# Transposing nine large groups by DMA, linear sums in four banks per group, coefficients without a clip, and a new order

## The chip, the core and the metric

The program runs on one core of one Trainium2 chip. The metric is the device time of one execution in microseconds (us), lower is better. One execution was profiled; its times, and a measured time beside its span, are what the numbers below come from.

## What is computed

`x` has 4 batches of 12480 rows of 128 values, `inducing` is 32 x 128. Per batch, 32 inducing rows attend over all 12480 rows (giving `h`, 32 x 128), then every row attends over the 32 rows of `h`, and the result goes through a two-layer network with a hard swish.

```python
def mab(q, kv):
    s = scale * (q @ kv.transpose(0, 2, 1))
    s = s - s.max(-1, keepdims=True)
    a = np.exp(s)
    a /= a.sum(-1, keepdims=True) + 1e-09
    return a @ kv
h = mab(I, x)                          # (4, 32, 128)
x2 = mab(x, h).reshape(49920, 128)
h2 = x2 @ w_in                         # w_in 128 x 2048
g = h2 * np.clip(h2 + 3.0, 0.0, 6.0) / 6.0
out = g @ w_out                        # 49920 x 128, float32
```

## The kernel before

A row's second attention is a weighted mean of 32 rows of `h`, so `h2` is the same mean of 32 rows of `G = h @ w_in`. While all of `G` lies within 3 of zero, the clip does nothing, and `out` is a quadratic form in the 32 weights: linear terms in the 32 weights squared by `e`, and products of two weights, with coefficients of 128 values each. The kernel computes per batch the coefficients (`Cq` for products, `BD` for linear terms) and per row the products, and multiplies. At the end it counts on the chip whether every assumption held (`y0` to `y5`, `bad_i`); if not, a slow direct path would run instead.

Rows of a batch come in **six large groups** of 2048 rows (g = 0 to 5) and one small group of 192 (g = 6). A large group is 16 tiles of 128 rows: 4 classes j by 4 tiles s. The program is written as a table of tokens, `ORDER`, a code with its arguments (batch b, group g, half h, PSUM bank k, engine V, A or P); the table alone sets the order on each engine, and each engine works through its own instructions strictly in that order. The eight PSUM banks are given by number in the tokens; the rings in SBUF by counting (`xh` 7, `xT` 13, `TF` 3, `TD` 2, `d` 3, `os` 2).

The steps of one large group, with the lines of before:

- `X` (L416, from POOL's queue): loads 2048 rows to `xh`, float32 to float16. `T` (L422): 8 transposes of 128 x 128 on TensorE for half a group, `Y` (L428): the copy of one bank to `xT` on DVE or ACT. `T` and `Y` stand twice per group.
- First attention: `S` (L433) scores, `E` (L441) exponential, `A` (L449, L459) sums, `H` (L476).
- After the last group of a batch, the coefficients: `c3` to `cB`, `G` (L523), `cG` (L532) writes `GL`, `cH` on POOL (L543) clips to `r6`, `cI` (L548) multiplies, `L`, `cL`, `cM`, `cm`, `cN` (L595, `BD` with a mask), `p` (L609), `P` (L616), `cP`, `cX`, `cY` (`Cq`). `cJ` (L553, DVE) takes the largest `G`.
- Second attention: `Z` (L656) scores, `Zz` (L678), `Zd` (L666), `Ze` (L671), `ee` (L692), `R`, `Rr`, `R2`. `W` (L698, four per group, SP's queue) copies `dk` to `d` with each partition's row on four partitions.
- Products, per half of a group: `B` (L731, tiles of 32 rows of the array, four banks), `F` (L741, ACT) to `TF`, `U` (L750, DVE) `TD = TF * d`.
- Sums: `q` (L789, 128 x 128 x 128 matmuls on `TF` and `TD`) and `l` (L770, tiles of 64 rows, 256 columns) into one bank for each half h and pair of classes jp, `v` (L807 on DVE, L811 on ACT) scales the bank's 512 columns into `os`, `O` (L817, SP's queue) stores `os`.

SP's queue thus holds `W` and `O`, POOL's queue `X` and the weights. Batches overlap: the first attention of batch b+1 stands among the products of batch b.

Of the kernel before, what the change touches and what calls it, by code (L numbers as in the profile page):

```python
# [9 lines left out]
FP32 = mybir.dt.float32  # L10
# [10 lines left out]
it X.0.1.0.16 i2 i1 w.2.0 i3.V T.0.1.0.8.1 Y.0.1.0.8.1.V i0 w.2.5 w.2.2 X.0.0.8.16 T.0.0.8.16.1 w.2.7 Y.0.0.8.16.1.V  # L21
i4.5 X.0.0.0.8 T.0.0.0.8.0 w.2.1 T.0.1.8.16.4 X.0.3.0.16 T.0.3.8.16.3 Y.0.0.0.8.0.A i5.5.V S.0.0.8.16.2 Y.0.1.8.16.4.A
X.0.2.0.16 T.0.3.0.8.0 Y.0.3.8.16.3.V Y.0.3.0.8.0.A E.0.0.8.16.2 S.0.0.0.8.6 i8 S.0.1.0.16.3 w.2.0 X.0.4.0.16 i6
A.0.0.8.16.7 H.0.0.8.16.7 T.0.2.0.8.2 w.2.1 E.0.0.0.8.6 A.0.0.0.8.6 w.2.4 T.0.2.8.16.4 Y.0.2.8.16.4.V Y.0.2.0.8.2.A
E.0.1.0.16.3 wi.0 wh.1.V A.0.1.0.16.2 S.0.3.0.16.3 E.0.3.0.16.3 X.0.5.0.16 T.0.4.0.8.0 Y.0.4.0.8.0.A H.0.1.0.16.2 i9
T.0.4.8.16.4 Y.0.4.8.16.4.V S.0.2.0.16.5 E.0.2.0.16.5 H.0.0.0.8.6 X.0.6.0.2 A.0.3.0.16.2 wh.0.A wl.0.V A.0.2.0.16.5
S.0.4.8.16.6 S.0.4.0.8.1 wi.1 T.0.5.8.16.4 T.0.6.0.2.3 T.0.5.0.8.0 E.0.4.0.8.1 Y.0.6.0.2.3.V S.0.6.0.2.7 Y.0.5.0.8.0.V
A.0.4.0.8.3 H.0.3.0.16.2 H.0.4.0.8.3 Y.0.5.8.16.4.A X.1.1.0.16 S.0.5.8.16.4 wh.2.V E.0.6.0.2.7 S.0.5.0.8.1 wh.3.V
E.0.5.8.16.4 X.1.0.0.16 wo.1 A.0.6.0.2.0 H.0.6.0.2.0 A.0.5.8.16.4 wo.0 E.0.4.8.16.6 A.0.4.8.16.7 H.0.5.8.16.4
E.0.5.0.8.1 H.0.4.8.16.7 H.0.2.0.16.5 A.0.5.0.8.6 H.0.5.0.8.6 c3.0.0 wl.3.V T.1.1.0.8.5 c7.0.V wl.1.P c8.0.V  # L30
T.1.1.8.16.4 i7.P G.0.1.2 wl.2.P G.0.3.2 G.0.2.2 Y.1.1.8.16.4.A c4.0.0 c9.0 cB.0.P G.0.0.2 cK.0 Z.0.2.1.7 Zd.0.2.7 cA.0
Z.0.0.0.1 Y.1.1.0.8.5.V cG.0.2 Z.0.0.1.5 Zd.0.0.5 W.0.0.0 W.0.0.2 Z.0.1.1.3 Zz.0.0.1 Z.0.1.0.2 Zd.0.1.3 Zz.0.1.2 W.0.0.1
cD.0.0.V T.1.0.8.16.0 T.1.0.0.8.4 X.1.3.0.16 cH.0.P cD.0.1.A Y.1.0.8.16.0.V S.1.1.0.16.6 Y.1.0.0.8.4.A W.0.0.3
E.1.1.0.16.6 Z.0.3.0.5 Z.0.2.0.7 cI.0 Zz.0.2.7 p.0.2.V W.0.2.3 B.0.0.0.2.0 S.1.0.0.16.4 F.0.0.0.0.2 E.1.0.0.16.4 L.0.0.6
A.1.1.0.16.7 W.0.2.0 H.1.1.0.16.7 L.0.1.6 cL.0.6 p.0.1.V A.1.0.0.16.4 cM.0.0.6 W.0.1.0 Ze.0.0 cm.0.3 ee.0.0.V cN.0.3
# [148 lines left out]
def kernel(  # L184
# [35 lines left out]
    with ExitStack() as es:  # L220
# [537 lines left out]
        def begins(b, g, h, jp):  # L758
            new = (b, g, h, jp) not in open_
            open_.add((b, g, h, jp))  # L760
            return new
# [269 lines left out]
```

## Time and profile before

| | |
|---|---|
| median of three timed runs (lowest, highest) | 249.86 us (248.54, 251.14) |
| the profiled execution, its time and its span | 249.51 us, 247.5 us |
| TensorE matmul (PE) busy | 227.0 us, 92% |
| VectorE (DVE) busy | 202.4 us, 82% |
| ScalarE (ACT) busy | 191.1 us, 77% |
| GpSimd (POOL) busy | 40.3 us, 16% |
| DMA | 53.91 MB, mean 218 GB/s |
| first and last `q` matmul | 47.4 us, 240.9 us |

A row of a group of instructions reads: line, engine, operation, out<-in, shapes, count, then busy us and mean ns of one, then the engine's idle time just before them and what ended it. A matmul's duration includes its way through the array; successive matmuls overlap, so what one costs is the distance from start to start. In a row of a window the columns are busy us with the number of instructions in brackets for PE, PE's weight loads (PEld), DVE, ACT and POOL, then the granted clock, the busy share of the DMA engines, and GB/s.

### The profile page before, as it was taken

How to read it: one execution, taken by the hardware profiler on the slowest of the kernel's cores; microseconds unless marked ns; L12 is line 12 of the kernel's file. 1: busy time of each engine (PE TensorE's matmuls, PEld its weight loads, DVE VectorE, ACT ScalarE, POOL GpSimd, SP SyncE). 2: the span in 40 equal slices, each digit the busy share in tenths (PEclk: the TensorE clock that was granted, in tenths of full speed). 3: DMA queues.
4: the chain of work that ended last, by engine and by line, in shares of the span. 5: the costliest groups of instructions: out<-in, count | busy, mean ns of one | idle time of the engine just before them, and what ended most of it. 6: DMA issues, size and time to landing. Idle time of an engine off the chain costs nothing. (4 is left out here: it accounts for less than half of the span.)

```text
span 247.5 us, 10076 instructions
## 1 busy us (share of the span) xinstructions
PE 227.0 (92%) x4317; PEld 186.5 (75%) x4317; DVE 202.4 (82%) x438; ACT 191.1 (77%) x350; POOL 40.3 (16%) x80
## 2 busy tenths in 40 slices
PE   1879799999799999999899999999999999989990
PEld 0568758888698798797787888888878877768780
DVE  0236879989599997999778998988889999998983
ACT  2167277998788886999687786999889889989870
POOL 8518582021002500010004000000031000000000
PEclk9999679999999999999999999999999999999998
DMA  6999789969989999849879974623981849696953
GB/s 96 193 255 254 238 158 193 208 163 250 214 286 263 277 196 331 293 87 250 184 252 265 266 274 110 224 56 76 338 305 37 262 97 340 211 311 170 362 232 134
DMA packets 23744, 53.91 MB, mean 218 GB/s; under 512 B 3697, under 2 KB 16785, under 8 KB 20753
## 3 DMA queue, kind: packets, MB, share of 16 engines
q1 hardware_dynamic: 19072, 38.36, 47.4%
q0 software_dynamic: 4624, 14.88, 31.0%
q8 instruction: 34, 0.56, 0.8%
q14 instruction: 14, 0.11, 0.1%
HBM read 27.67 MB, written 25.56 MB: 215 GB/s over the span
## 5 line engine op out<-in xcount | busy, mean ns | idle before, releaser
L741 ACT ACTIVATE TF<-ps 128x1024 f16<-128x1024 f32 (+1 forms) x100 | 96.8, 1007 | 16.1 <-PE ps L731 12.4
L750 DVE TENSOR_TENSOR TD<-TF,d 128x2048 f16<-128x2048 f16 (+1 forms) x52 | 59.9, 1156 | 3.0 <-ACT TF L741 2.2
L789 PE MATMUL ps<-Cq,TF 128*128 128x128 f16 (+1 forms) x784 | 57.9, 219 | 2.6 <-issue 1.4
L789 PE MATMUL ps<-Cq,TD 128*128 128x128 f16 (+1 forms) x784 | 56.0, 219 | 0.0
L807 DVE TENSOR_TENSOR os<-ps,r 128x512 f32<-128x512 f32 x68 | 45.4, 683 | 11.7 <-PE ps L789 4.1
L789 PEld LDWEIGHTS <-TF 128*128 128x128 f16 (+1 forms) x784 | 46.3, 98 | 6.3 <-issue 6.0
L789 PEld LDWEIGHTS <-TD 128*128 128x128 f16 (+1 forms) x784 | 46.1, 99 | 4.3 <-issue 3.4
L811 ACT ACTIVATE os<-ps,r 128x128 f32<-128x128 f32 x112 | 32.0, 380 | 4.3 <-PE ps L789 2.0
L422 PE MATMUL ps<-ident_h,xh 128*128 128x128 f16 x384 | 29.8, 226 | 5.5 <-DMA xh<-in_x_dram 5.5
L422 PEld LDWEIGHTS <-xh 128*128 128x128 f16 x384 | 24.0, 102 | 11.6 <-DMA xh<-in_x_dram 7.5
L428 DVE COPY xT<-ps 128x1024 f16<-128x1024 f16 x31 | 21.2, 684 | 12.8 <-PE ps L422 12.5
L428 ACT COPY xT<-ps 128x1024 f16<-128x1024 f16 x17 | 17.0, 1015 | 18.9 <-PE ps L422 18.8
L416 POOL DMA_DIRECT2D xh<-in_x_dram x25 | 13.9, 560 | 75.1 <-PE ps L459 62.2
L731 PE MATMUL ps<-z,pair 32*128 32x256 f16 (+1 forms) x400 | 20.3, 270 | 0.0
L609 DVE TENSOR_TENSOR PR<-Gd 128x2048 bf16<-128x2048 bf16 x16 | 19.8, 1239 | 0.0
L678 DVE TENSOR_SCALAR_CACHE_REDUCE z<-ps 128x512 f16<-128x512 f32 (+1 forms) x28 | 17.3, 621 | 2.4 <-PE ps L656 2.3
L666 ACT ACTIVATE dk<-ps 128x512 f16<-128x512 f32 (+1 forms) x28 | 14.8, 547 | 5.5 <-PE ps L656 3.4
L770 PE MATMUL ps<-BD,ee 64*128 64x256 f16 (+1 forms) x196 | 17.5, 273 | 0.2
L441 ACT ACTIVATE a<-ps 128x512 f16<-128x512 f32 (+1 forms) x27 | 14.6, 556 | 2.6 <-PE ps L433 2.6
L616 PE MATMUL ps<-w_ob,PR 128*128 128x128 bf16 x256 | 16.5, 219 | 0.0
L671 ACT ACTIVATE e<-z 128x512 f16<-128x512 f16 (+1 forms) x28 | 16.3, 589 | 0.1
L616 PEld LDWEIGHTS <-PR 128*128 128x128 bf16 x256 | 14.7, 98 | 0.9 <-issue 0.8
(137 smaller groups left out, 284.8 us busy)
## 6 DMA issues: line engine op xcount, KB each, us to landing
out_dram<-os SPq DMA_DIRECT2D x23, 1024.0 KB, 5.2
d<-dk SPq DMA_DIRECT2D x96, 128.0 KB, 3.9
xh<-in_x_dram POOLq DMA_DIRECT2D x23, 512.0 KB, 8.8
os<-in_moe_w_in_dram POOLq DMA_DIRECT2D x2, 512.0 KB, 13.4
w_or<-in_moe_w_out_dram POOLq DMA_DIRECT2D x2, 512.0 KB, 11.6
out_dram<-os SPq DMA_DIRECT2D x2, 512.0 KB, 3.6
xh<-in_x_dram POOLq DMA_DIRECT2D x2, 256.0 KB, 7.3
out_dram<-osl SPq DMA_DIRECT2D x4, 96.0 KB, 3.0
```

The source lines that it names most:

```text
L422: nc.tensor.transpose(pt[:, (i - lo) * p : (i - lo + 1) * p], at(xh, xhl, b, g)[:p, i, :], ident_h[:p, :p])
L428: copier(e)(xT_of(b, g)[:, lo * p : hi * p], ps[:, k, :].bitcast(FP16)[:, : (hi - lo) * p])
L609: veng(e).tensor_mul(pr_of(b, c)[:, :, :].rearrange("p a (i m) -> p a i m", m=M), views[0], views[1])
L616: nc.tensor.matmul(ps[:, k, f * C : (f + 1) * C], lhsT=pr_of(b, c)[:, jb, :], rhs=w_ob[:, jb, :], start=first_of(b, u), stop=False, skip_g ...
L678: nc.vector.tensor_scalar(fat(z_, b, g)[:rows, :w], ps[:rows, k, :w], 1.0, None, op0=ALU.mult, op1=ALU.min, accum_out=z_all[:rows, b * NGR ...
L731: nc.tensor.matmul(ps[:, pairs[j // 2] + j % 2, f * w : (f + 1) * w], lhsT=pair[rows, f, :], rhs=fat(z_, b, g)[rows, h * w : (h + 1) * w], ...
L741: nc.scalar.activation(hat(TF_, b, g, h)[:, 2 * q : 2 * q + 2, :w], ps[:, k : k + 2, :w], ACT.Exp, scale=scale / KH)
L750: nc.vector.tensor_mul(split(hat(TD_, b, g, h)), split(hat(TF_, b, g, h)), d.unsqueeze(2).to_broadcast([P, J, 2, w]),)
L770: nc.tensor.matmul(ps[:p, ks[jp], s2 * 2 * C : (s2 + 1) * 2 * C], lhsT=fat(e2_, b, g)[rows, s * p : (s + 1) * p], rhs=BD_[b % 2][rows, :, ...
L789: nc.tensor.matmul(ps[:p, k, (s2 * 2 + j2) * C : (s2 * 2 + j2 + 1) * C], lhsT=t[:, j, f * w + s2 * p : f * w + (s2 + 1) * p], rhs=Cq_[b % ...
L807: nc.vector.tensor_mul(o, src, r.unsqueeze(3).to_broadcast([p, Sh, 2, C]))
L811: nc.scalar.mul(o[:, s2, j2, :], src[:, s2, j2, :], r[:, s2, j2 : j2 + 1])
```

## The change

It does four things.

1. **Transposes by DMA.** For nine of the 24 large groups (2.1, 2.3, 2.4, 2.5, 3.1 to 3.5; batch and group) the two `T` and two `Y` go, and one token `t` comes: a DMA transpose of the whole group, `xh` to `xT`, in SP's queue. 18 of 48 large `T` and `Y` go: 15 of those `Y` stood on DVE, 3 on ACT.
2. **Linear sums of a whole group.** `l` is called once per large group: 16 matmuls of 32 rows and 128 columns, one array tile and one bank for each class j, in place of two calls of 4 matmuls of 64 rows and 256 columns. `q` writes each class to its own bank, so a group's sums stand in four banks, both halves side by side, until a `v` per class reads 512 columns.
3. **No clip.** `cH` and `r6` go, `cI` computes (G + 3) G at once; `cJ` becomes a sum of squares on ACT (with the bound 9 in place of 3 on the largest). The mask in `BD` goes.
4. **New order.** `ORDER` is another table; matmuls that only keep TensorE awake are 12 in place of 16, and seven copies to `Gd` stand on ACT in place of four.

The core of the diff:

```diff
 ORDER = """
-... T.2.3.8.16.3 ... Y.2.3.8.16.3.V ...
+... t.2.3 ...
+        def op_t(b, g):
+            nc.sync.dma_start(
+                xT_of(b, g)[:, :].rearrange("c (i t) -> c i t", t=P),
+                at(xh, xhl, b, g)[:, :, :].rearrange("t i c -> t (i c)"),
+                transpose=True,
+            )
...
-        def op_cH(b, e):
-            veng(e).tensor_scalar(
-                r6[:, :, :], GL[:, :, :M].bitcast(FP32), 3.0, 0.0, op0=ALU.add, op1=ALU.max
-            )
-
         def op_cI(b):
             nc.vector.scalar_tensor_tensor(
-                GL[:, :, M:], r6[:, :, :], 6.0, GL[:, :, :M].bitcast(FP32), op0=ALU.min, op1=ALU.mult
+                GL[:, :, M:],
+                GL[:, :, :M].bitcast(FP32),
+                3.0,
+                GL[:, :, :M].bitcast(FP32),
+                op0=ALU.add,
+                op1=ALU.mult,
             )
 
         def op_cJ(b):
-            nc.vector.tensor_reduce(
-                g_all[:, b : b + 1],
+            nc.scalar.activation(
+                junk[:, :].rearrange("p (a m) -> p a m", m=M),
                 GL[:, :, :M].bitcast(FP32),
-                axis=AX.XY,
-                op=ALU.max,
-                apply_absolute_value=True,
+                ACT.Square,
+                accum_out=g_all[:, b : b + 1],
             )
...
+        def op_l(b, g, *ks):
+            t0, p, J, Sn = groups[g]
+            for s in range(Sn):
+                for j in range(J):
+                    rows = slice(32 * j, 32 * j + 32)
                     nc.tensor.matmul(
-                        ps[:p, ks[jp], s2 * 2 * C : (s2 + 1) * 2 * C],
+                        ps[:p, ks[0] + j if g == NG else ks[j], s * C : (s + 1) * C],
                         lhsT=fat(e2_, b, g)[rows, s * p : (s + 1) * p],
-                        rhs=BD_[b % 2][rows, :, :].rearrange("p j c -> p (j c)"),
-                        start=begins(b, g, h, jp),
+                        rhs=BD_[b % 2][rows, :],
+                        start=begins(b, g, j),
                         stop=False,
                         skip_group_check=True,
-                        tile_position=(64 * jp, 0),
+                        tile_position=(32 * j, 0),
                     )
...
-        def op_q(b, g, h, jp, u, k):
+        def op_q(b, g, h, jp, u, *ks):
...
-                            ps[:p, k, (s2 * 2 + j2) * C : (s2 * 2 + j2 + 1) * C],
+                            ps[:p, ks[0] + j2 if g == NG else ks[j2], (h * Sh + s2) * C : (h * Sh + s2 + 1) * C],
...
-        def op_v(b, g, h, jp, k, e):
+        def op_v(b, g, j, k, e):
...
-                nc.vector.tensor_mul(o, src, r.unsqueeze(3).to_broadcast([p, Sh, 2, C]))
+                n = js.stop - js.start
+                nc.vector.tensor_mul(o, src, r.unsqueeze(3).to_broadcast([p, n, Sn, C]))
```

**SP's queue while batch 1 is multiplied out.** The first piece is of before, from the store of group 0.5 on; L698 is `W` (`d`), L817 is `O` (`os`), 96 at a row's end is the small group.

```order
L817 DMA out_dram<-os_118 128x2048
L698 DMA d_111<-dk_108 128x1x512 x2
L698 DMA d_110<-dk_107 128x1x512 x2
L698 DMA d_109<-dk_106 128x1x512
L698 DMA d_111<-dk_108 128x1x512 x2
L698 DMA d_110<-dk_107 128x1x512
L817 DMA out_dram<-os_117 128x2048
```

The second piece is of the change, from the store of group 0.5 on as well; L694 is `W`, L813 is `O`, and L423 is `t` (here of groups 2.3 and 2.4).

```order
L813 DMA out_dram<-os_118 128x2048
L423 DMA_TRANSPOSE xT_79<-xh_69 128x16x128
L423 DMA_TRANSPOSE xT_80<-xh_70 128x16x128
L694 DMA d_109<-dk_106 128x1x512 x3
L694 DMA d_110<-dk_107 128x1x512 x2
L813 DMA out_dram<-os_117 128x2048
```

Two transposes now stand between the store and the `W` of groups 1.2 and 1.3.

**DVE while groups 2.0 and 2.1 are multiplied out.** The first piece is of before: L807 is `v`, L428 is `Y` (`xT_85` to `xT_87` are groups 3.3 to 3.5), L750 is `U` of group 2.1, L692 is `ee`.

```order
L807 TENSOR_TENSOR os_117<-ps,r_165 128x2x256
L428 COPY xT_85<-ps 128x1024
L807 TENSOR_TENSOR os_117<-ps,r_165 128x2x256
L692 TENSOR_TENSOR ee_102<-e_99 128x512
L428 COPY xT_85<-ps 128x1024
L750 TENSOR_TENSOR TD_115<-TF_113,d_109 128x2048
L428 COPY xT_86<-ps 128x1024
L807 TENSOR_TENSOR os_117<-ps,r_165 128x2x256
L428 COPY xT_87<-ps 128x1024
```

The second piece is of the change, at the same groups: L800 is `v`, L746 is `U` of group 2.1, L475 is `H`, L688 is `ee`, L719 is `R2`.

```order
L800 TENSOR_TENSOR os_117<-ps,r_163 128x4x128 x2
L475 TENSOR_TENSOR hacc_135<-hacc_135,ps 128x33
L800 TENSOR_TENSOR os_117<-ps,r_163 128x4x128 x2
L746 TENSOR_TENSOR TD_115<-TF_113,d_109 128x2048
L475 TENSOR_TENSOR hacc_135<-hacc_135,ps 128x33
L746 TENSOR_TENSOR TD_116<-TF_114,d_109 128x2048
L688 TENSOR_TENSOR ee_100<-e_97 128x512
L688 TENSOR_TENSOR ee_102<-e_99 128x512
L719 TENSOR_TENSOR r_163<-rc_162 128x16
L800 TENSOR_TENSOR os_118<-ps,r_163 128x4x128 x4
```

The copies to `xT` are gone, and the four evictions of group 2.1 (`os_118`) stand in one run, where before those of group 2.0 (`os_117`) stood one by one between copies.

More of the change, by code (lines that the diff above doesn't have):

```diff
@@ L26 @@
[L26 to L35, printed above, removed]
@@ L153 @@
+q.3.5.1.1.0.4.5 l.3.5.0.1.4.5 W.3.6.0 y2 B.3.6.0.6 v.3.4.1.2.A O.3.4.0.16 q.3.5.0.0.1.0.1 cJ.3 q.3.5.1.0.0.0.1
+q.3.5.1.0.1.0.1 F.3.6.0.0.6 Ze.3.6 ee.3.6.V R2.3.5.V v.3.5.0.0.A v.3.5.1.1.V q.3.5.0.1.1.4.5 U.3.6.0 q.3.5.1.1.1.4.5
+q.3.5.0.1.0.4.5 R.3.6.7 Rr.3.6.7 O.3.5.0.8 v.3.5.3.5.V R2.3.6.V y1 q.3.6.0.0.1.2 q.3.6.0.0.0.2 v.3.5.2.4.A O.3.5.8.16
+l.3.6.2 v.3.6.0.2.V y0 O.3.6.0.2 y3 y4.6 y5.6
 """
@@ L247 @@
         Cq_ = ring("Cq", 2, [P, 4, C], FP16)
-        BD_ = ring("BD", 2, [P, 2, C], FP16)
+        BD_ = ring("BD", 2, [P, C], FP16)
         HS_ = ring("HS", 2, [P, M], FP16)
@@ L258 @@
         Gd = sb.tile([P, FB, 2 * M], BF16, name="Gd")
-        r6 = sb.tile([P, FB, M], FP32, name="r6")
         LV = sb.tile([2 * M, C], FP32R, name="LV")
@@ L279 @@
         ones = sb.tile([P, 1], FP32, name="ones")
-        mask = sb.tile([P, 2, C], FP16, name="mask")
         fac = sb.tile([P, 4], FP32, name="fac")
@@ L351, in op_i6 @@
                 e.memset(blk[rows, j : j + 1], math.sqrt(KC))
-                e.memset(mask[rows, j % 2, :], 1.0)
             e.memset(fac[:, :], KC / 3.0)
@@ L756, with begins @@
         open_ = set()
-        def begins(b, g, h, jp):
-            new = (b, g, h, jp) not in open_
-            open_.add((b, g, h, jp))
+        def begins(b, g, j):
+            new = (b, g, j) not in open_
+            open_.add((b, g, j))
             return new
-        def op_l(b, g, h, *ks):
+        def op_l(b, g, *ks):
             t0, p, J, Sn = groups[g]
-            Sh = (Sn + 1) // 2
-            for s2 in range(Sh):
-                s = h * Sh + s2
-                for jp in range(J // 2):
-                    rows = slice(64 * jp, 64 * jp + 64)
+            for s in range(Sn):
+                for j in range(J):
+                    rows = slice(32 * j, 32 * j + 32)
                     nc.tensor.matmul(
-                        ps[:p, ks[jp], s2 * 2 * C : (s2 + 1) * 2 * C],
+                        ps[:p, ks[0] + j if g == NG else ks[j], s * C : (s + 1) * C],
                         lhsT=fat(e2_, b, g)[rows, s * p : (s + 1) * p],
-                        rhs=BD_[b % 2][rows, :, :].rearrange("p j c -> p (j c)"),
-                        start=begins(b, g, h, jp),
+                        rhs=BD_[b % 2][rows, :],
+                        start=begins(b, g, j),
                         stop=False,
                         skip_group_check=True,
-                        tile_position=(64 * jp, 0),
+                        tile_position=(32 * j, 0),
                     )
-        def op_q(b, g, h, jp, u, k):
+        def op_q(b, g, h, jp, u, *ks):
             t0, p, J, Sn = groups[g]
@@ L816, in op_O @@
             r0 = b * N + t0
-            nc.sync.dma_start(
-                out[r0 : r0 + p * n, :].rearrange("(p i) c -> p i c", i=n)[:, lo:hi, :],
-                at(os_, osl, b, g)[:p, lo:hi, :],
-            )
+            o = out[r0 : r0 + p * n, :].rearrange("(p i) c -> p i c", i=n)
+            t = at(os_, osl, b, g)[:p]
+            if hi - lo == n:
+                nc.sync.dma_start(o, t)
+            else:
+                half = lambda a: a.rearrange("p (s j) c -> p s j c", j=J)[:, :, lo // 4 : hi // 4, :]
+                nc.sync.dma_start(half(o), half(t))
         def op_dr():
@@ L844, in op_y3 @@
         def op_y3():
-            count(3, g_all[:, :], 3.0, ALU.is_le)
+            count(3, g_all[:, :], 9.0, ALU.is_le)
             d = d_all[:, :, :].rearrange("p b m -> p (b m)")
```

269 lines of the change are left out of this document (133 added, 136 removed).

## The prediction

> **What bounds the kernel now.** I read the page's busy shares first, then busy time by stretch, then who waits for whom, then single instructions in one stretch.
>
> ```profile
> PE 227.0 (92%) x4317; PEld 186.5 (75%) x4317; DVE 202.4 (82%) x438; ACT 191.1 (77%) x350; POOL 40.3 (16%) x80
> ```
>
> The stretches are the head (up to the first `q`), two parts of the long middle stage, and the tail after the last `q`. Columns: PE, PEld, DVE, ACT, POOL, then granted clock, DMA share, GB/s.
>
> ```profile
> 0.00:47.00 47.00, 37.06 (x685) 29.12 (x686) 27.20 (x66) 25.44 (x39) 24.70 (x58) 0.93 0.93 200
> 47.00:200.00 153.00, 149.78 (x2956) 124.76 (x2953) 135.53 (x283) 128.56 (x243) 15.56 (x22) 1.00 0.78 216
> 200.00:241.00 41.00, 39.79 (x680) 32.46 (x676) 37.41 (x71) 36.46 (x69) 0.00 (x0) 1.00 0.76 257
> 241.00:247.50 6.50, 0.39 (x7) 0.14 (x5) 2.29 (x22) 0.62 (x2) 0.00 (x0) 0.84 0.40 149
> ```
>
> In the 194 us from 47 to 241, PE is busy 149.8 + 39.8 = 189.6 us (98%), DVE 172.9 (89%), ACT 165.0 (85%). The head has the fullest DMA engines (0.93).
>
> The longest waits of PE:
>
> ```profile
> PE ps L422 <- DMA xh<-in_x_dram: 5.5, 3, 4.3
> ...
> PE ps L854 <- DVE junk L831: 1.9, 1, 1.9
> ...
> PE ps L481 <- DVE hacc L476: 1.5, 1, 1.5
> ```
>
> They lie in the head, the tail and before the coefficients. So the middle stage is **bound by TensorE's own work**, with DVE and ACT close behind; whatever leaves PE there counts until one of those two sets the pace.
>
> **The change, part by part.**
>
> *Transposes that leave PE.* Durations overlap, so the price is the distance between starts, taken from runs of 8 and 16:
>
> ```profile
> 19.45 1.05 PE L422 MATMUL ps<-ident_h,xh 128*128 128x128 f16 x16
> ...
> 23.18 0.61 PE L422 MATMUL ps<-ident_h,xh 128*128 128x128 f16 x8
> ```
>
> Eight more take 0.44 us, 55 ns each. Nine groups of 16 are 144: **7.9 us** off PE, all in the middle stage.
>
> *Linear sums.* One stretch of PE's rows shows both ways:
>
> ```profile
> 228.97 0.28 PE L731 MATMUL ps<-z,pair 32*128 32x256 f16 x4
> 229.18 0.39 PE L770 MATMUL ps<-BD,ee 64*128 64x256 f16 x4
> 229.51 0.62 PE L789 MATMUL ps<-Cq,TF 128*128 128x128 f16 x8
> 229.96 0.24 PE L704 MATMUL ps<-blk,e 128*128 128x4 f16 x4
> 230.07 1.05 PE L789 MATMUL ps<-Cq,TD 128*128 128x128 f16 x16
> 231.05 0.61 PE L770 MATMUL ps<-BD,ee 64*128 64x256 f16 x8
> 231.60 0.40 PE L731 MATMUL ps<-z,pair 32*128 32x256 f16 x8
> 231.93 0.45 PE L789 MATMUL ps<-Cq,TD 128*128 128x128 f16 x5
> ```
>
> `l` before costs 229.51 - 229.18 = 0.33 us for one half alone, 231.60 - 231.05 = 0.55 us for both together: 0.55 to 0.66 us per group, about 0.60. The new shape, 16 matmuls on four tiles of 32 rows, is not in the trace. Its nearest row is `B` (L731), also four tiles of 32 rows: 8 matmuls of 256 columns in 0.33 us, way out included, as many columns per tile as the 16 of 128. That is the fast end, 0.33. The slow end: 4-column `R` matmuls (L704) start (230.07 - 229.96)/4 = 27 ns apart, so 16 starts that cannot overlap take 0.43, and with the 0.2 us that `B` needs until the next full-size matmul 0.63. I take 0.40, near `B`. Per group 0.20 less, times 24: **4.8 us**, bounds (0.55 - 0.63) x 24 = -1.9 and (0.66 - 0.33) x 24 = 7.9. Together PE loses 12.7 us (6.0 to 15.8). Four warm-up matmuls fewer lie in the head, where PE waits for loads: nothing.
>
> *Evictions and small work.*
>
> ```profile
> L428 DVE COPY xT<-ps 128x1024 f16<-128x1024 f16 x31 | 21.2, 684 | 12.8 <-PE ps L422 12.5
> ...
> L428 ACT COPY xT<-ps 128x1024 f16<-128x1024 f16 x17 | 17.0, 1015 | 18.9 <-PE ps L422 18.8
> ...
> L807 DVE TENSOR_TENSOR os<-ps,r 128x512 f32<-128x512 f32 x68 | 45.4, 683 | 11.7 <-PE ps L789 4.1 <-DMA out_dram<-os 3.5 <-ACT TF L741 2.9
> ...
> L811 ACT ACTIVATE os<-ps,r 128x128 f32<-128x128 f32 x112 | 32.0, 380 | 4.3 <-PE ps L789 2.0 <-PE ps L770 1.1 <-ACT e L671 1.0
> ...
> L553 DVE TENSOR_REDUCE g_all<-GL 128x1 f32<-128x512 f32 x4 | 2.7, 665 | 0.0
> ...
> L641 ACT ACTIVATE junk<-Cp 128x512 f32<-128x512 f16 x4 | 2.5, 635 | 0.0
> ...
> L540 ACT CAST Gd<-GL 128x512 bf16<-128x512 f32 x4 | 2.4, 618 | 1.2 <-DVE GL L532 1.2
> ...
> L543 POOL TENSOR_SCALAR r<-GL 128x512 f32<-128x512 f32 x4 | 8.6, 2143 | 7.1 <-DVE GL L532 4.1 <-DVE r L723 2.8 <-DVE hm L506 0.3
> ```
>
> DVE: 15 copies at 0.684 (-10.3), `cJ` (-2.7), two large `v` more (+1.4), about -11.6 us. ACT: 3 copies (-3.0), two large `v` fewer (8 x 0.38 = -3.0), four squares at `cQ`'s price (+2.5), three `Gd` copies (+1.9): -1.6 us. So after the change the middle stage holds about PE 176.9, ACT 163.4, DVE 161.3. The clip on POOL (8.6 us) stood between `GL` and `cI`; PE has batch work beside it (98% busy), so I count nothing, and at most 2.1 us for batch 0.
>
> *What this makes of the stage.* At PE's 98% it would take 180.5 us, 13.5 less. But ACT would then be at 91%, and in the stretch from 200 to 241, where no transposes stand and all three engines are fullest, ACT reaches 36.46/41 = 89% and DVE 91%. At 89% for ACT the stage takes 163.4/0.89 = 183.6 us, 10.4 less. I take 9.5, since four banks per group leave PE a little less room (the second rival).
>
> *The transposes in SP's queue.* Each `t` waits for its load and stands ahead of `W` and `O`, which wait behind it; behind `W` wait `U` and then `q` on `TD`.
>
> ```profile
> q1 hardware_dynamic: 19072, 38.36, 47.4%
> q0 software_dynamic: 4624, 14.88, 31.0%
> ...
> out_dram<-os SPq DMA_DIRECT2D x23, 1024.0 KB, 5.2
> d<-dk SPq DMA_DIRECT2D x96, 128.0 KB, 3.9
> ...
> out_dram<-os SPq DMA_DIRECT2D x2, 512.0 KB, 3.6
> ```
>
> The trace has no DMA transpose. A group is 512 KB. By q1's bytes (38.36 MB in 47.4% of 16 x 247.5 us, 20.4 KB per us and engine) it holds all 16 engines 1.6 us. By q1's packets (98 ns each), if it goes as 2048 pieces of 256 bytes, 2048 x 98/16 = 12.6 us. The nearest row is the 512 KB store, 3.6 us from issue to landing; I take 3 us of all engines. Nine are 27 us (14 to 113). The two queues use 78.4% of 247.5, 194 us, so the stretch from 47 to 200, 0.78 full, has 0.22 x 153 = 34 us free: 27 fit. Below 34 us the term is nothing.
>
> The Trainium skill speaks twice here. "VectorE: DVE Perf Modes", section "The three transpose paths", gives 390 ns for a 128 x 128 block on TensorE and 1309 ns by DMA, which speaks against the change; as an estimate 16 blocks would be 20.9 us, nine groups 188 us. "Advanced Engine Details and Errata", section "X-Bar Transpose (TRN2)", says that such DMAs are as fast as ordinary ones, 350 to 400 GB/s; as an estimate 1.4 us per group. By the second the term above stays nothing; by the first the first rival comes. The trace cannot decide: of the 390 ns it shows 55 in a run, since a block alone is not a block in a row, and the same may hold for the DMA.
>
> *Head and tail.* Batch 0 is loaded in another order, as many bytes ahead of its last group, with the DMA engines as full: nothing, within 2 us. The tail is the same chain of counts.
>
> *Sum.* 249.5 (247.5 span and 2.0 around it) - 9.5 = **240.0 us**. The profiled execution lies 0.35 us under the median of 249.86, which I leave out.
>
> **Rivals.**
>
> *The transposes fill the DMA engines (slower).* For it: the engines are 0.93 busy in the head and 0.78 in the stretch that gets the nine; SP already issues in bursts on the chain that ended last, two of whose issues and the store behind them are
>
> ```profile
> 172.74 0.62 SPq L698
> ...
> 173.40 0.60 SPq L698
> ...
> 174.05 5.95 DMA out_dram<-os
> ...
> 180.09 0.69 DVE os L807
> ```
>
> and DVE's eviction there waits for the store. Against it: 34 us are free, and 512 KB need 1.6 us by bytes. Past 34 us every us lengthens the stage; it turns slower than before at (34 + 9.5)/9 = 4.8 us of all engines per transpose. At 6 us: 240 + (54 - 34) = 260; at 12.6: 240 + 79 = 319.
>
> *Four banks filled and emptied together (gain gone).* Before, a bank closed after 16 `q` and its `l`; now four stay open over both halves, and `B` and `F` of the next half take the other four, so PE may wait for an eviction, 0.683 us. Once in each of 24 groups that is 16.4 us: 249.5 - 12.7 + 16.4 = 253; in every second group 245. For it: DVE's evictions now stand in runs of four. Against it: `Z`, `S`, `A` and the other group's `q` stand in between.
>
> *The gain in full.* ACT and DVE keep up at 91%, `l` is at 0.33, the clip's 2.1 us goes: 249.5 - 13.5 - 1.7 - 2.1 = 232.
>
> That nothing happens because the transposes stay on PE is excluded: nine stand in SP's queue.
>
> **Chances.** Forecast, 236 to 244: 0.44. Gain in full, under 236: 0.20. Banks, 244 to 252: 0.20. DMA engines, above 252: 0.16. The range of 231 to 252 leaves out the last case and a little below. A measurement here tells no less than about 1% from no change, so the bounds are 247.4 and 252.4: of the bank case three fifths lie above 247.4. Faster 0.44 + 0.20 + 0.08 = 0.72, same 0.12, slower 0.16.
>
> **What would show it.** The transposes: 240 matmuls of 128 x 128 left on L414's line, a landing time of 3 to 6 us for `xT<-xh`, and a DMA share between 47 and 200 below 0.95. The linear sums: from the first of 16 to the next instruction 0.33 to 0.45 us. The bound: PE still above 95% in the middle, ACT near 89%. The forecast is wrong if PE waits for `xT` before scores (late transposes), if SP stands long at a `t`, if the rows of PE's waits name `v` (L800, L804), or if the stage before the first `q` grows.

## The result, and the profile after

The change is slower: 264.13 us median (262.96 to 267.94) beside 249.29 of the kernel before on the same chip (248.54 to 251.14), ratio 1.057, 95% interval 1.047 to 1.067. The forecast was 240.0, the range 231 to 252. The profiled execution took 267.94 us, span 265.8. Ratios compare only executions within 1.5% of their kernel's fastest, while medians take all of them; the profiled executions of the change, of the kernel with no `t` and of some others lie above that.

The page's first line, and the middle in three stretches (columns as in the prediction: PE, PEld, DVE, ACT, POOL, granted clock, DMA share, GB/s). First the kernel before, in shorter stretches than the prediction looked at:

```profile
47.00:100.00 53.00, 51.63 (x1021) 44.03 (x1019) 45.99 (x96) 44.52 (x83) 7.53 (x12) 1.00 0.95 245
100.00:150.00 50.00, 48.80 (x984) 40.34 (x980) 44.48 (x92) 40.75 (x75) 4.85 (x7) 1.00 0.81 227
150.00:200.00 50.00, 49.35 (x963) 40.39 (x960) 45.06 (x98) 43.29 (x86) 3.18 (x3) 1.00 0.56 174
```

Then the change:

```profile
PE 219.5 (83%) x4365; PEld 184.2 (69%) x4365; DVE 192.3 (72%) x414; ACT 191.9 (72%) x352; POOL 30.3 (11%) x72
```

```profile
47.00:100.00 53.00, 41.07 (x790) 34.40 (x790) 33.30 (x74) 34.18 (x66) 3.45 (x8) 0.90 0.89 209
100.00:150.00 50.00, 43.42 (x956) 37.02 (x948) 38.95 (x81) 38.47 (x74) 3.12 (x7) 0.97 1.04 236
150.00:200.00 50.00, 44.33 (x881) 37.61 (x880) 38.13 (x78) 38.49 (x72) 1.22 (x1) 0.89 1.01 230
```

PE did lose work, but it now waits: 24 of the 153 us are idle, where 3 were, and around its idle spells the granted clock is lower (0.74 between 140 and 160 us, around a wait of 6.5 us), so that busy time holds less work. The DMA engines are full between 100 and 200. The free time that the prediction counted (0.22 of 153 us) lay almost all behind 100 us: between 47 and 100 the engines were 0.95 busy in the kernel before.

The queues, the landings, and all instructions of the line of `t` (durations min/median/max in ns, landings in us):

```profile
q1 hardware_dynamic: 38560, 43.08, 60.8%
...
out_dram<-os SPq DMA_DIRECT2D x23, 1024.0 KB, 5.9
d<-dk SPq DMA_DIRECT2D x96, 128.0 KB, 4.1
...
xT<-xh SPq DMA_TRANSPOSE x9, 10.3
```

```profile
L423 SPq DMA_TRANSPOSE xT<-xh x9: 3457/5687/12397, 77.5 to 178.2; - x9
...
DMA to landing us min/median/max: 5.5/10.3/16.0
```

A transpose lands 10.3 us after issue, not 3 to 6. What the prediction did not price at all is the duration in the row of L423: SP itself is held 5.7 us by one `t` in the median (60.3 us by nine), where a `W` or a store holds it 0.5 to 0.6 in the median. The single packets in the trace show 2048 pieces of 256 bytes per transpose, 36 ns each in the mean (18 in the median): 41.5 us of all 16 engines for nine, 4.6 each.

What comes of it, at one place: SP's queue, then ACT and DVE (start, duration, in brackets the idle time before and what ended it), then the waits of the whole run:

```profile
132.93 5.69 SPq L423 DMA_TRANSPOSE xT<-xh  x1
138.67 5.28 SPq L694 DMA_DIRECT2D d<-dk  x7
```

```profile
150.96 0.60 ACT L662 ACTIVATE dk<-ps 128x512 f16<-128x512 f32 x1 [7.06 <-DMA d<-dk]
```

```profile
151.00 1.23 DVE L746 TENSOR_TENSOR TD<-TF,d 128x2048 f16<-128x2048 f16 x1 [5.84 <-DMA d<-dk]
```

```profile
DVE TD L746 <- DMA d<-dk: 14.0, 5, 5.8
...
ACT dk L662 <- DMA d<-dk: 9.5, 2, 7.1
...
PE ps L783 <- ACT dk L662: 6.5, 1, 6.5
```

The `t` of group 3.1 holds seven `W` back by 5.7 us. ACT, whose `Zd` may not overwrite `dk` before the `W` has read it, and DVE's `U` wait for them, and PE's next `q` waits for ACT: 6.5 us, the longest wait of PE behind the first `q`. The hold is not all of it. The `t` itself had landed at 140.5 us, but as the `W` went out, three loads did too (POOL's queue), and the seven `W` landed 10.2 us after issue, where 4.1 is the median of the run:

```profile
140.62 1.63 POOL L408 DMA_DIRECT2D xh<-in_x_dram  x3
```

```profile
d<-dk SPq DMA_DIRECT2D x7, 128.0 KB, 10.2
```

Held back, the `W` ran into the loads; how much of the wait is hold and how much is the burst, this place alone does not show.

### The profile page after: what moved, and what is told of

It reads as the page before. It is cut to its first block, busy times and chain, and to the rows that moved or that the text cites. A ratio compares the mean times of both kernels' runs of the same rounds, so it can differ in the third digit from the quotient of the medians.

```text
span 265.8 us, 10173 instructions
## 1 busy us (share of the span) xinstructions
PE 219.5 (83%) x4365; PEld 184.2 (69%) x4365; DVE 192.3 (72%) x414; ACT 191.9 (72%) x352; POOL 30.3 (11%) x72
## 3 DMA queue, kind: packets, MB, share of 16 engines
q1 hardware_dynamic: 38560, 43.08, 60.8%
## 5 line engine op out<-in xcount | busy, mean ns | idle before, releaser
L746 DVE TENSOR_TENSOR TD<-TF,d 128x2048 f16<-128x2048 f16 (+1 forms) x52 | 59.2, 1148 | 18.4 <-DMA d<-dk 14.0
L783 PE MATMUL ps<-Cq,TF 128*128 128x128 f16 (+1 forms) x784 | 59.7, 225 | 7.3 <-ACT dk L662 6.5
L800 DVE TENSOR_TENSOR os<-ps,r 128x512 f32<-128x512 f32 x70 | 45.7, 683 | 23.7 <-DMA out_dram<-os 9.3
L783 PE MATMUL ps<-Cq,TD 128*128 128x128 f16 (+1 forms) x784 | 58.7, 222 | 1.1 <-DVE TD L746 0.6
L783 PEld LDWEIGHTS <-TF 128*128 128x128 f16 (+1 forms) x784 | 48.5, 101 | 11.7 <-issue 10.9
L783 PEld LDWEIGHTS <-TD 128*128 128x128 f16 (+1 forms) x784 | 46.8, 100 | 9.1 <-issue 6.8
L804 ACT ACTIVATE os<-ps,r 128x128 f32<-128x128 f32 x104 | 29.6, 383 | 7.1 <-DMA out_dram<-os 4.3
L420 ACT COPY xT<-ps 128x1024 f16<-128x1024 f16 x14 | 14.0, 1014 | 16.6 <-PE ps L414 16.5
L414 PE MATMUL ps<-ident_h,xh 128*128 128x128 f16 x240 | 19.6, 237 | 7.4 <-DMA xh<-in_x_dram 7.1
L727 PE MATMUL ps<-z,pair 32*128 32x256 f16 (+1 forms) x400 | 22.6, 274 | 2.4 <-ACT dk L662 2.0
L662 ACT ACTIVATE dk<-ps 128x512 f16<-128x512 f32 (+1 forms) x28 | 15.1, 560 | 10.3 <-DMA d<-dk 9.5
L414 PEld LDWEIGHTS <-xh 128*128 128x128 f16 x240 | 16.0, 107 | 8.6 <-DMA xh<-in_x_dram 7.2
L420 DVE COPY xT<-ps 128x1024 f16<-128x1024 f16 x16 | 10.9, 685 | 12.2 <-PE ps L414 12.2
L432 PE MATMUL ps<-I_T,xT 128*128 128x32 f16 x384 | 13.8, 178 | 1.3 <-ACT xT L420 0.5
```

What stands on the lines that cost most here:

```text
L414: nc.tensor.transpose(pt[:, (i - lo) * p : (i - lo + 1) * p], at(xh, xhl, b, g)[:p, i, :], ident_h[:p, :p])
L420: copier(e)(xT_of(b, g)[:, lo * p : hi * p], ps[:, k, :].bitcast(FP16)[:, : (hi - lo) * p])
L727: nc.tensor.matmul(ps[:, pairs[j // 2] + j % 2, f * w : (f + 1) * w], lhsT=pair[rows, f, :], rhs=fat(z_, b, g)[rows, h * w : (h + 1) * w], ...
L746: nc.vector.tensor_mul(split(hat(TD_, b, g, h)), split(hat(TF_, b, g, h)), d.unsqueeze(2).to_broadcast([P, J, 2, w]),)
L783: nc.tensor.matmul(ps[:p, ks[0] + j2 if g == NG else ks[j2], (h * Sh + s2) * C : (h * Sh + s2 + 1) * C], lhsT=t[:, j, f * w + s2 * p : f * ...
L800: nc.vector.tensor_mul(o, src, r.unsqueeze(3).to_broadcast([p, n, Sn, C]))
```

## Experiments

The prediction left two kinds of cause: the transposes themselves, and the rest of the change. Ratios are to the kernel before, timed beside each; "SP" is the time that all issues of SP's queue took in the profiled execution, "pieces" what the replaced transfers took of all 16 DMA engines.

| kernel | median us | ratio (95%) | SP, us | pieces, us |
|---|---|---|---|---|
| before | 249.3 | 1 | 89.6 | - |
| the change | 264.1 | 1.057 (1.047 to 1.067) | 162.2 | 41.5 |
| no `t` | 253.8 | 1.019 (1.012 to 1.025) | 101.2 | - |
| a plain copy in 4 KB rows for `t` | 251.1 | 1.006 (1.001 to 1.011) | 115.0 | 12.0 |
| a plain copy in 256-byte pieces | 260.1 | 1.045 (1.038 to 1.053) | 148.8 | 21.6 |
| the same pieces from ACT's queue | 257.1 | 1.026 (1.019 to 1.034) | 108.5 | 22.4 |
| ten tiny copies for each `t` | 279.8 | 1.124 (medians) | 165.3 | 0.9 |
| no `t`, late loads | 245.6 | 0.985 (0.978 to 0.992) | 102.4 | - |

### What the transposes cost, and what the rest is worth

```diff
 def op_t(b, g):
-    nc.sync.dma_start(..., transpose=True)
+    pass
```

> The nine t are left out, with nothing in their place: those nine groups' rows are not transposed, S and Z read what an earlier group left in xT. Everything else of the change stays, its order too. If the transposes are the whole cause (by filling the DMA engines or by holding SP's queue), this gives what the rest of the change is worth: 236 to 244 us. If the four banks or the new order eat the gain, it stays above 252, and PE's waits still name v (L800, L804 by their numbers in the change).

253.76 us: between the two. Without any transposing of nine groups, on TensorE or by DMA, the rest of the change is still 1.9% **slower** than before, where the sum had it 9.5 us faster. So, left out in this way, the transposes cost about 3.8% (9.5 us), and the rest has a loss of its own. Windows and waits of this kernel (profiled execution 258.1 us), then its stores between 70 and 100 us with their landing time:

```profile
47.00:100.00 53.00, 40.81 (x729) 34.75 (x727) 30.80 (x62) 32.05 (x60) 2.11 (x4) 0.83 0.71 190
100.00:150.00 50.00, 49.86 (x1123) 42.85 (x1119) 43.99 (x97) 45.54 (x87) 4.50 (x10) 1.00 0.81 217
150.00:200.00 50.00, 49.66 (x1060) 42.84 (x1057) 46.35 (x98) 45.80 (x90) 1.72 (x2) 1.00 0.74 230
```

```profile
DVE os L796 <- DMA out_dram<-os: 9.0, 1, 9.0
PE ps L696 <- DVE os L796: 7.9, 2, 7.5
```

```profile
out_dram<-os SPq DMA_DIRECT2D x3, 1024.0 KB, 14.3
```

From 100 us on PE is over 99% busy with four banks per group. The loss lies before: DVE waits 9.0 us for one store that lands 14.3 us after issue, and PE behind it 7.5. In POOL's queue three loads went out at 74 us, beside these stores, and five between 36 and 44 us, when the first `W` are due.

Four replacements for `t` at its place in SP's queue, to part its load from its place:

```diff
-    nc.sync.dma_start(..., transpose=True)
+    for n in range(10):                                                  # ten tiny copies
+        nc.sync.dma_start(xT_of(b, g)[:16, n * P : n * P + 8], at(xh, xhl, b, g)[:16, n, :8])
```

> Each t is replaced by ten tiny copies from xh to xT (16 partitions of 16 bytes) at its place in SP's queue: the same waits for the load and for the slot in xT, and SP held for about 10 x 0.6 = 6 us, as the median t holds it 5.7 us, but only 160 small packets. The rows are not transposed. If holding SP's queue, with W and O behind it, is the cause: 255 to 264 us, and U waits for d as in the change (14 us). If the load on the DMA engines is the cause: within 3 us of the kernel with no t.

279.75, worse than the change: holding SP, with next to nothing on the DMA engines, is enough to cost 26 us over no `t`. (The ten held SP 5.5 to 9.1 us a place, more than was meant, and with the waits between them a place took up to 13.3 us. So a hold alone can cost more than the whole loss, but this run does not give the price of a transpose's hold.)

```diff
-    nc.sync.dma_start(..., transpose=True)
+    nc.sync.dma_start(xT_of(b, g)[:, :].rearrange("c (i t) -> c i t", t=P),
+                      at(xh, xhl, b, g)[:, 0:1, :].to_broadcast([P, TG, C]))
```

> Each t is replaced by one plain copy in SP's queue that writes as much to the same xT in 2048 pieces of 256 bytes (the first tile of the group sixteen times; nothing is transposed). If what costs is 2048 small packets, 36 ns each in the mean as with t: 4.6 us of all 16 engines each and a time near 264. If the transpose itself is what stops other transfers: 256-byte pieces run at their median of 18 ns or less beside others, 2.3 us of all engines each, 21 us for nine, within the 34 us free before, and the time is within 4 us of the kernel with no t. SP's issue time for it shows whether SP is held by the number of pieces (about 5.7 us again) or not (0.6).

260.14. The pieces run at 19 ns, so the load is half that of `t`, and SP's own issue of it takes 0.6 us; but the transfers issued behind it take longer, SP's sum grows by 48 us over no `t`, and most of the 3.8% is there. The transpose as such adds about 1% (1.057 for 1.045; the intervals overlap).

```diff
+    nc.sync.dma_start(xT_of(b, g)[:, :], at(xh, xhl, b, g)[:, :, :].rearrange("t i c -> t (i c)"))
```

> Each t is replaced by one plain copy of the same 512 KB from xh to xT in rows of 4 KB, at the same place in SP's queue (nothing is transposed). By the queue's bytes it needs 1.6 us of all 16 engines, nine 14 us. This is the transfer that the prediction had in mind with its 3 us. If load by bytes or the place in the queue were the cause it lies well above the kernel with no t; if the transposes' own pace is the cause, within 3 us of it.

251.11, 1.3% below no `t`, which neither case said. The transfer that the prediction had in mind is indeed free, at the same place and with the same waits for its load.

```diff
-    nc.sync.dma_start(...256-byte pieces...)
+    nc.scalar.dma_start(...256-byte pieces...)
```

> Each t is replaced by the plain copy in 2048 pieces of 256 bytes, now issued from ACT's queue (nothing is transposed). The same load as with these pieces in SP's queue (260 us, 4.5% above before), but W and O do not stand behind them; ACT issues each in about 0.6 us, 6 us in all, and may wait for a load. If W and O held in SP's queue are what the pieces cost: 252 to 256 us, as with no t, and SP's issues sum to about 105 us in place of 149. If the load on the DMA engines is: 258 to 263.

257.10, ratio 1.026: from ACT's queue the same load costs 0.8% over no `t`, from SP's 2.7%, and SP's issues are back at 108.5 us. So about two thirds of what the pieces cost is what they hold up in SP's queue, a third (within its interval nothing) their load, as far as ACT's order sends them at times that compare. The same with `t` itself:

```diff
-    nc.sync.dma_start(..., transpose=True)
+    nc.scalar.dma_start(..., transpose=True)
```

> The change with the nine t issued from ACT's queue in place of SP's: the same pieces and load, but W and O no longer stand behind them. If W and O held in SP's queue are most of what the transposes cost (10 to 12 us): 253 to 259 us, and U's wait for d falls from 14 to below 7 us. If the load on the DMA engines is, or if holding ACT costs as much: 262 us or more.

280.21. The case above 262 came, but it named two causes, load and a held ACT, and this run does not part them. The row shows that a transpose holds ACT too (31.7 us by nine; behind one of them ACT stood idle for 9.0 us):

```profile
L423 ACTq DMA_TRANSPOSE xT<-xh x9: 1447/2545/10066, 87.4 to 186.3; - x9
```

```diff
-... t.2.3 ... t.2.5 ...   # all four of batch 2
```

> The change with the four t of batch 2 left out (those rows are not transposed) and the five of batch 3 kept. With no t it was 1.9% above before, with nine 5.7%. If every transpose costs the same: 1.9 + 5/9 x 3.8 = 4.0% above before, 259 us. If the first four, which stand between 77 and 123 us where the DMA engines are fullest, cost nearly all: 254 to 256. If the last five do, in front of the W of batch 2: 262 to 264.

262.57, ratio 1.052 (1.044 to 1.060): five of the nine give nearly all of it. They go out between 128 and 172 us here, ahead of the `W` of batches 1 and 2, and not where the DMA engines of the kernel before were fullest.

```diff
-... t.2.5 ...
+... t.2.5.0.4 ... t.2.5.4.8 ... t.2.5.8.12 ... t.2.5.12.16 ...   # two to three W or O between
```

> The change with each t cut into four transposes of four tiles, two to three of SP's other transfers standing between them where the next step leaves room. The same 2048 pieces of 256 bytes per group, so the same load on the DMA engines (41.5 us of all 16 in sum), but SP is held for about a quarter as long at a time. If what costs is W and O held behind a t: 254 to 259 us. If it is the load on the DMA engines: 262 to 266.

283.65, which neither case gave. The parts, spread towards the scores, came too late for them (`S` waited 20.6 us for `xT`), so this says little of the hold.

The first part alone, on the kernel before:

```diff
-... T.2.3.0.8.0 ... Y.2.3.0.8.0.V ... T.2.3.8.16.3 ... Y.2.3.8.16.3.V
+... t.2.3 ...
```

> The kernel before with part 1 alone: for the same nine groups the T and Y go, and t stands where the first T of the group stood; its order, its two banks per half, its clip stay. If the transposes cost more than they take from PE wherever they stand: 252 to 262 us (8 us less on PE, 10 to 12 us or more for the transposes, since U and v wait). If the transposes are cheap and the change's own order is the whole trouble: 240 to 244 us.

295.60 beside 249.56, far worse than expected. One transpose meets four loads there, and for 39 us hardly anything moves (SP's queue, then the window):

```profile
78.73 7.99 SPq L428 DMA_TRANSPOSE xT<-xh  x1
86.78 38.78 SPq L702 DMA_DIRECT2D d<-dk  x7
```

```profile
82.00:121.00 39.00, 8.71 (x152) 7.44 (x150) 7.23 (x12) 5.77 (x18) 2.83 (x3) 0.62 1.04 81
```

The DMA engines count as busy (1.04) at 81 GB/s.

### The transpose by itself

Trials behind the last store of the kernel with no `t`, with nothing else running:

```diff
+m.0 m.0 m.1 m.2 m.3 m.4 m.0 m.5        # e7: t, t, 4 tiles, 1 tile, pieces, rows, t, t from ACT
+m.t m.tx m.tO m.px m.x m.t m.tW m.pO m.O   # pairs: t, p pieces, x a load, O a store, W
+m.xct m.xcp ...                        # three loads, three tiny copies, then t or p
+m.xt m.xdt m.xddt m.xdddt ...          # three loads, 0 to 3 multiplications, then t or p
```

> The kernel with no t, and behind its last store, with nothing else on the DMA engines, one after the other: two transposes of a whole group, one of four tiles, one of one tile, a plain copy of a group's size in 2048 pieces of 256 bytes, one in rows of 4 KB, a third whole transpose, and one from ACT's queue. Its time as a whole is not compared. If the transposes are slow by themselves: a whole group holds SP about 3.5 us (the shortest in the change) and lands 4.5 to 6 us after issue, its pieces still at 36 ns. If they are slow only beside other transfers: 2.3 us of all engines (18 ns a piece, as the plain copy), SP held below 2 us, landing in 3 to 4 us.

> The kernel with no t, and behind its last store a row of trials with nothing else running: a whole transpose alone, a transpose beside one load (from POOL's queue, 2048 rows to float16), a transpose behind a 1 MB store in SP's queue, the plain copy in 2048 pieces alone, the same beside a load, a load alone, a transpose alone, four W and a transpose, the store and the plain copy, the store alone. A small copy on POOL between them waits until all has landed. Its time as a whole is not compared. If a transpose and other traffic hinder each other: its pieces at 18 ns alone, 50 to 200 ns beside the load or the store, and the pair takes more than the two one after the other (load alone plus transpose alone); the plain copy in pieces stays at 19 ns beside the same load. If they only share the engines: the pair takes no longer than the sum, with pieces at 18 to 25 ns.

Alone, a whole transpose holds SP 1.4 to 2.0 us and its pieces run at 22 ns; the first row is the shortest hold (L443). The plain copy in pieces holds SP 0.65 us alone and 0.67 beside a load (L449), at 19 ns a piece. POOL's copy behind the transpose starts 4.4 us after issue:

```profile
282.83 1.35 SPq L443 DMA_TRANSPOSE xT<-xh  x1
```

```profile
268.67 0.67 SPq L449 DMA_DIRECT2D xT<-xh  x1
```

```profile
287.23 0.19 POOL L429 COPY gate<-xT 128x1 f16<-128x1 f16 x1 [4.31 <-DMA xT<-xh]
```

Behind a store the transpose holds SP 4.7 us. From first to last packet it takes 2.6 us alone, with a load 6.0 (a load alone 3.4), with a store 5.5 (a store alone 2.8): sharing, not hindering.

> The kernel with no t, and behind its last store trials with nothing else running: three loads alone; three loads with a transpose issued some 5 us later (three tiny copies one after the other delay it), so that its pieces fall among the loads' packets; three loads with the plain copy of 2048 pieces in the same place; the tiny copies and a transpose alone; the three loads with the transpose again; three loads alone. Its time as a whole is not compared. If a transpose moves in lockstep over the 16 engines and waits for the slowest each time: pieces and loads stretch (pieces over 100 ns in the mean, 4 KB packets over 500 ns), and three loads with the transpose take over 18 us where the sum is about 9 + 2.6. If they only share: about 12 us, pieces at 18 to 30 ns, as with the plain copy.

The tiny copies took some 5 us each beside the loads, so the transposes came after them; inconclusive.

> The kernel with no t, and behind its last store trials with nothing else running: three loads alone (8.3 us from the first to the last packet by the trial before); three loads and a transpose at once; the same with the transpose held back by one, two and three multiplications on DVE (about 1.2 us each); three loads with the plain copy in 2048 pieces held back by two and by three. Its time as a whole is not compared. Lockstep: where its pieces meet the loads' packets, pieces of 0.3 us and more end together and the pair takes 14 us and more, with 4 KB packets far over their 0.34 us. Sharing: 8.3 + 2.6 = 11 us, pieces at 18 to 30 ns, loads' packets at 0.34 us, as with the plain copy.

Three loads and a transpose take 10.8 to 11.1 us from first to last packet, pieces at 20 to 22 ns: the sum again, so the lockstep beside loads that the expectation names does not show. But SP is held 6.6 to 7.7 us by a transpose behind loads, by the plain copy 0.6. The first of these trials, issue to landing:

```profile
xT<-xh SPq DMA_TRANSPOSE x1, 11.2
```

So 10 us to land and 6 us of SP are what a transpose takes once its pieces queue behind loads or stores. Its time on the engines stays short in these trials, though: 22 ns a piece, where the whole kernel has 36 in the mean. The last section shows where that time is.

### The bursts of loads

```diff
-... X.2.0.0.16 ... X.1.5.0.16 ... X.1.4.0.16 ... X.2.1.0.16 ...
+... X.1.4.0.16 ... gt.0.0 X.1.5.0.16 X.2.0.0.16 ... gt.0.1 X.2.1.0.16 ... gt.0.2 X.2.2.0.16 ...
+def op_gt(b, g):
+    nc.gpsimd.tensor_copy(gate[:, g : g + 1], fat(d_, b, g)[:, 0, :1])
```

> As the kernel with no t, but eight loads of batches 1 and 2 are held back: group 1.5 and 2.0 until the last W of group 0.1 has landed, then one load per W of the next group (a small copy on POOL that reads d stands before each), with 1.4 ahead of 1.5. With no t the loads came in bursts: five between 36 and 44 us, when W of group 0.0 has to come through, and three at 74 us beside two stores, when DVE then waited 9.0 us for a store and PE 7.5 us for DVE. If these bursts are why the rest of the change brings nothing: 237 to 243 us, DVE's wait for the store below 3 us and the first U before 52 us (56.7 with no t). If the four banks or the order of the sums are why: 249 to 254, as with no t.

245.57, ratio 0.985: 8 us less than with no `t`, two to three short of what was expected. The first `U` is back at 46.8 us (45.6 before, 54.0 with no `t`; the 56.7 of the expectation is the second `U`), and the 9 us wait is gone:

```profile
47.00:100.00 53.00, 48.54 (x955) 40.47 (x956) 41.41 (x87) 42.38 (x81) 6.70 (x17) 0.94 0.87 213
100.00:150.00 50.00, 49.86 (x1083) 43.44 (x1081) 44.40 (x91) 45.17 (x88) 2.64 (x6) 1.00 0.86 246
150.00:200.00 50.00, 49.51 (x1044) 41.81 (x1043) 45.99 (x98) 46.62 (x90) 1.72 (x2) 1.00 0.69 220
```

> The change as it is, all nine t included, with the late loads. The late loads took 8 us off the kernel with no t. If bursts of loads and transposes add up: 255 to 258 us. If later loads now run into the transposes of 2.5, 2.1, 2.3 and 2.4 and both crawl, as the first transpose did for 39 us in the kernel before with transposes alone: 264 us or more.

The whole change with the same late loads: 268.16 (259.46 to 273.57) beside 249.64. The runs spread too far to say whether the gain adds up with the transposes; the lowest is below the change's 262.96, the median above its 264.13.

A whole kernel without transposes by DMA, in the hope of one faster than both:

```diff
-... t.2.3 ...
+... T.2.3.0.8.2 ... Y.2.3.0.8.2.V ... T.2.3.8.16.4 ... Y.2.3.8.16.4.A ...   # with the late loads
```

> A whole kernel without transposes by DMA: the change's order and its other parts with the late loads, and the nine groups' rows transposed on TensorE and copied on DVE and ACT again (twelve copies DVE, six ACT), each T at a place where a bank is free for 1.3 to 4 us. The late loads alone, with nothing for the transposes, gave 245.6. The transposes put back 7.9 us on PE, 8.2 on DVE and 6.1 on ACT: 250 to 254 if PE sets the pace, so no better than before; below 247 only if PE had that much room.

267.85, worse than expected: PE's share between 100 and 200 falls to 90%. Which of the places for `T` cost this is open. As an estimate, 245.6 with the transposes nowhere and the 7.9 us that they take on PE make 253.5, if PE sets the pace, so better places would hardly have beaten 249.

What lets the loads go early? The clip on POOL, part 3, stood ahead of them in POOL's queue:

```diff
 # e16, on the kernel before            # e18: cI as here, cH stays
-    veng(e).tensor_scalar(r6[...], GL[...], 3.0, 0.0, op0=ALU.add, op1=ALU.max)   # cH
+    pass
-    nc.vector.scalar_tensor_tensor(GL[:, :, M:], r6[...], 6.0, GL[...], op0=ALU.min, op1=ALU.mult)
+    nc.vector.scalar_tensor_tensor(GL[:, :, M:], GL[...], 3.0, GL[...], op0=ALU.add, op1=ALU.mult)
```

> The kernel before with the clip alone taken out: cI multiplies (G + 3) G at once and POOL's cH goes; order, banks, transposes and cJ stay. The prediction counted nothing for it and at most 2.1 us. If PE's other work covers the coefficients: within 0.4% of before. If batch 0's chain sets the start of the products: 1.5 to 2.5 us less, 247 us; this would then be a version faster than both.

258.17, ratio 1.024 (1.018 to 1.030): slower, which neither case said.

> The kernel before; cI multiplies (G + 3) G at once, and the clip still runs on POOL, but nothing reads what it writes. If the kernel without the clip is slower because POOL's loads went out 2 to 3 us earlier: as before, within 0.6%. If it is slower because the coefficients come earlier, or for another reason in DVE's order: 254 to 258 again.

251.01 beside 251.37, ratio 1.001 (0.996 to 1.006). With the clip's result unused but POOL busy, nothing changes; so it is the 2 us of POOL each time, not the coefficients. POOL's queue before and without the clip (profiled execution 260.2 us), each with its window from 80 to 90:

```profile
81.50 1.98 POOL L543 TENSOR_SCALAR r<-GL 128x512 f32<-128x512 f32 x1 [0.27 <-DVE hm L506]
83.45 0.58 POOL L416 DMA_DIRECT2D xh<-in_x_dram  x1
```

```profile
80.00:90.00 10.00, 10.00 (x195) 8.49 (x192) 9.83 (x22) 9.36 (x24) 4.29 (x6) 1.00 1.05 255
```

```profile
81.88 0.54 POOL L416 DMA_DIRECT2D xh<-in_x_dram  x1
```

```profile
80.00:90.00 10.00, 8.30 (x129) 6.52 (x126) 7.13 (x15) 5.96 (x13) 2.36 (x5) 0.83 1.05 254
```

One load 1.6 us earlier, DMA engines full either way, and PE stands for 1.7 us with its clock down. That the load is the way from POOL to PE fits these rows; it was not tried apart. Nor is this all of the loss: between 100 and 150 PE is busy 45.1 us for 48.8, which these rows do not explain.

## Why the prediction was wrong, step by step

The measured time lies 24 us above the forecast. By the kernel with no `t`, about 10 of them are the transposes (264.1 to 253.8) and 14 the rest of the change (253.8 to 240.0). Late loads took 8 of the 14 back; the other 6 stay open.

- *PE loses 12.7 us* held in sum. With late loads PE is busy 214.7 us for 227.0, 12.3 less. `l` was put too high: by the distance of its starts it takes 0.29 us per group there (7.06 us for 384 matmuls, 14.81 for 192 before), below even the 0.33 of the fast end, where 0.40 was taken. (In the change it is 9.76 us, with 2.60 of waiting in it.)
- *DVE -11.6, ACT -1.6*: DVE 192.3, 10.1 less; ACT 191.9, 0.8 more. 1.5 us off on DVE, 2.4 on ACT; neither decides.
- *The transposes in SP's queue* is **the step that failed**. "Below 34 us the term is nothing" priced them by the time on all engines alone. That was 41.5 us for nine, over the 27 taken and the 34 free; and the hold in the queue (60 us at `t`, against 5 for nine ordinary transfers), which the text only named as a sign to look for, had no price, though `W` stands behind it and PE behind `W`. The free time was an average over 153 us of a stretch that was 0.95 full in its first third; but the five `t` of batch 3, which stand behind that third, cost nearly all, so the missing price of the queue weighs more.
- *Head and tail, nothing within 2 us*, and *the clip, nothing*, **failed too**, and by the split above the rest of the change weighs more than the transposes: 14 us, 8 of them the bursts of loads of the new order. The first `U` came at 50.8 us for 45.6, and in the kernel before the clip's 2 us on POOL were worth 2.4%, most likely because they held loads back. What "hides" an edit was sought on PE; it lay in a queue.
- *The stage at ACT's 89%* was never reached, so "whatever leaves PE there counts" did not hold. Even with late loads and no transposes anywhere the span fell 3.5 us for 12.3 us of PE's work: idle time of PE grew by 8.8, 3.4 before 47 us and 3.1 between 47 and 100.
- *Rivals.* The first (0.16) came as a slower kernel, and its point of decision, 4.8 us, lies beside the 4.9 by which the first queue grew per transpose (60.8% of 16 x 265.8 us in the change, 45.8% of 256.1 with no `t`: 44.3 us in nine). But by its own sum 4.9 us each give 240 + (44 - 34) = 250. That the 260 it named for 6 us lies near 264 is luck: most of what the pieces cost is the hold and not the load, and the loss of the new order is not in it. Four banks are cleared: without `t`, PE is over 99% busy from 100 to 200.
- *The two pages.* The Trainium skill's "Advanced Engine Details and Errata", section "X-Bar Transpose (TRN2)", has such a transfer as fast as an ordinary one. From first to last packet, with nothing else running, the transpose took 2.6 us, the plain copy in as many pieces 2.5, the plain copy in 4 KB rows 1.4: as fast as the one, not as the other. The 1309 ns a block in the Trainium skill's "VectorE: DVE Perf Modes", section "The three transpose paths", do not carry over to a batch: 16 blocks landed in 4.3 us alone.

## What to carry to other kernels

Price a new transfer three times: on the DMA engines, in the queue that issues it (a transpose holds its issuer, behind a store or loads all the more, and plain pieces of 256 bytes hold what stands behind them), and by its landing, in the stretch where it stands and not in the mean. An order tuned to the microsecond holds loads back by accident as well as by design: before taking work off an idle engine, see which transfers that work stands ahead of.

## What the runs showed of the hardware

A transpose of 512 KB within SBUF holds its issuing engine 1.4 to 2.0 us alone, 4.7 behind a store, 6.6 to 7.7 behind three loads, up to 12.4 in the kernel. A plain copy in as many pieces holds it 0.6, but passes the wait on: with nine of them in SP's queue, the issues of `W` took 121.2 us in place of 83.4.

In the whole kernel the pieces of a transpose stretch in groups: ten times, 10 to 21 pieces at once last over 0.8 us (1.1 to 2.6 in the median of a group) and end within 0.1 us of each other. Together with one group of three this is 16.8 of the 41.5 us. Five of the ten groups came as one 16 KB fetch of instructions was running (the one at 88.9 us with nothing else beside it), four beside 8 KB packets of stores, one beside loads. The plain copies in as many pieces met eight such fetches from ACT's queue, and none of their pieces lasted over 0.13 us. In the trials with three loads no fetch met a transpose, and no piece lasted over 0.36 us. So in these runs the pieces of a transpose stopped together where those of a plain copy did not; why is open. What all DMA engines of the change move from 88 to 91 us, in 40 slices, with the gap from 89 to 90.3:

```profile
GB/s 17 17 34 20 92 403 273 273 263 283 270 259 31 20 17 0 0 0 0 0 7 10 7 7 10 10 7 14 10 7 10 24 273 283 294 297 280 297 290 287
```

Once, beside loads, a transpose crawled for 39 us at 81 GB/s. This did not come back in the trials with three loads; its cause stays open.
